# A fused convolution and gated feed-forward kernel: another order of the unit products, another start, and a split last product

## The chip, the cores and the metric

The kernel runs on one core of one Trainium2 chip. The metric is the device time of one execution in microseconds (us), the median of several runs. The core has five engines that work side by side, each with its own in-order queue of instructions: TensorE (PE, matmuls; PEld is its weight load), VectorE (DVE), ScalarE (ACT), GpSimd (POOL) and SyncE (SP, which here issues most DMAs). Matmuls write to PSUM, which has 8 banks of 128 partitions x 512 fp32 numbers.

## The reference

The input x is (8, 4096, 192), fp32. First comes a causal convolution along the sequence with 7 taps, whose weights are a softmax over the taps, one set for each of 8 groups of 24 channels. Then a feed-forward layer follows with a gate between two products:

```python
w = np.exp(w - max); w = w / (sum + 1e-09)
out = np.einsum('hk,bskhg->bshg', w, x_unf)
h = x @ w_in                        # (32768, 192) @ (192, 2048)
g = h * np.clip(h + 3.0, 0.0, 6.0) / 6.0
return g @ w_out                    # (32768, 2048) @ (2048, 192)
```

The weights w_in and w_out arrive as 64-bit numbers and are turned into fp32 on the chip.

## The kernel before, in words

**Blocks.** The 32768 tokens are worked on in 32 blocks of 1024. The 192 channels lie as 64 partitions x 3 "thirds"; partitions 0 to 63 hold the lower 512 tokens of a block, 64 to 127 the upper 512. So a product of the first layer needs 64 rows of TensorE's array, and the lower half (called L, k=0) and the upper half (U, k=1) run side by side on the two halves of its rows (`half_mm`, L303). Such a product is two passes over 512 columns. "OWN" is y, the result of the convolution, in place; "OTHER" is y with the two halves exchanged by DMA (`swap`, L273), so that each half of the rows can also work on the other half's tokens.

**First layer, blocks 1 to 31** (`h_phase`, L404). The layer is done by a scheme of Strassen's kind: seven products P1 to P7 on sums of y (YS1 to YS4, `y_sums`) and of weights (w_in_t), and four plain products K11, K12, K21, K22 for the remaining third. 16 column blocks of w_in make 8 slots, two slots a unit, so 4 units (UNITS), each once for L and once for U. Products of one result add up in one PSUM bank: bank a holds P1, P2, K11; e holds P5; b begins as a copy of P1 and takes P6, P7, P4, K21; f begins as b + p5 and takes P3, K12; d begins as b + p5 and takes K22. A step's name is L or U and an operation: a product; F1, ScalarE's copy of bank a into b (L385), made between P1 and P2 and needed by P6; CE, ScalarE's copy of bank e to SBUF (L388), which gives the bank back; AF and AD, VectorE's sums into f and d (L392); Ra, Rf, Rb, Rd, ScalarE's relu of a result (L317); Ga and so on, VectorE's gate, which writes g and gives the bank back (L321). The string PLAN (L349) is the order in which every unit's steps are issued, and so the order in each engine's queue; a step with ' belongs to the unit before. X (only the first time) is the last store of the block before. Banks are handed out first in, first out (`take`, `give`), so the order of the steps sets which bank a step waits for. After each round GpSimd forms sums of g (`g_sums`).

**Second layer** (`out_strassen`, L586; `out_last`, L546, for the last block). It is of Strassen's kind too: products of 32 output columns each, four side by side on the columns of the array (L427), each over all 128 rows and all 8 slots, two passes each. ScalarE and VectorE (L523, L531) combine the results, VectorE transposes (L537), and SP, at the very end ScalarE too, stores. During this stage VectorE also computes the next block's convolution (L259, L263), and the exchange goes out.

**Block 0** is plain. Its start (from L643) computes the convolution with third 2 on TensorE (diagonal matrices, L661) and thirds 0 and 1 on VectorE in half-width taps, and turns the weights into fp32 unit by unit between: `split` (VectorE, L174 and L178), `clamp` (ScalarE, L186 to L192), `join` (VectorE, L195 and L199, then a GpSimd product, L203). Four pairs of banks are begun early with thirds 0 and 2 (`early`), then third 1. Loop L707 relus and gates; `slots` (L705) says behind which of its 16 steps a weight unit is worked on. Then `out_direct` (L450) does the second layer plainly.

Of the kernel before, what the change touches and what calls it, by code (L numbers as in the profile page):

```python
# [16 lines left out]
def kernel(  # L17
# [316 lines left out]
    def h_out(c, group, bs, between):  # L334
# [14 lines left out]
    PLAN = """  # L349
        LP1 LRd' UP1 LGd' LP4' UP4' URd' LF1 LP5 UGd' UF1 UP5 LP6 UP6 LP2 LCE UCE LRb'  # L350
        UK11 LAF UAF LK11 X URb' UP2 LP7 LGb' UP7 LK12 UP3 UGb' LAD LP3 LRa URa LRf UK12
        UAD UGa LGa LK22 UK22 URf LGf UGf LK21 UK21
    """.split()

# [49 lines left out]
    def h_phase(left):  # L404
        last = None
        for u in range(UNITS + 1):
            now = [Unit(u, k) for k in range(2)] if u < UNITS else None
            for step in PLAN:
                if step == "X":
                    while left:  # L410
                        left.pop(0)()
                    continue
                which = last if step[-1] == "'" else now
                if which:
                    which["LU".index(step[0])].run(step[1:].rstrip("'"))
            if last:
                g_sums(nc.gpsimd, (1, 3), range(2 * u - 2, 2 * u), 2)
            last = now
# [4 lines left out]
    def mm(bank, j, x, w, q, ps_, first, last):  # L423
# [4 lines left out]
                out=bank[j * QS : (j + 1) * QS], lhsT=w_out[:, p, w, cols], rhs=x[:, p],  # L428
# [13 lines left out]
    def store_rows(i, k, q, xt, j, dma=nc.sync):  # L442

        t0 = i * TB + k * N
        dma.dma_start(
            out=out[t0 : t0 + N, q * QS : (q + 1) * QS].rearrange("(t r) d -> r t d", r=QS),
            in_=xt[j * QS : (j + 1) * QS].rearrange("r (t d) -> r t d", d=QS),
        )
# [46 lines left out]
    def product(bank, j, n, q, ks=every):  # L495
        x, w = prod[n]
        return mm(bank, j, S1 if n == 5 else x, w, q, ks, True, True)
# [35 lines left out]
    def store(i, c, k, half_, qs=range(NQ), queues=(nc.sync,)):  # L533
# [3 lines left out]
        nc.vector.transpose(out=xt[r], in_=c[r])  # L537
        for q in qs:
            store_rows(i, k, half_ * NQ + q, xt, q, queues[q % len(queues)])
# [6 lines left out]
    def out_last(i):  # L546
# [32 lines left out]
        b, bank = three(3, 4, 2)  # L579
        add(u2[:], u2[:], bank[m])  # L580
        store(i, u2, 0, 1, queues=both)
        add(u3[rows(2)], u3[rows(2)], bank[rows(NQ)], ALU.subtract)
        store(i, u3, 1, 0, range(2, 3), queues=both[::-1])
        give(b)
# [58 lines left out]
    with tc.manual_schedule():  # L643
# [6 lines left out]

        thirds = [slice(s, s + 1) for s in range(K3)]
        pe_third = K3 - 1
        b = take()
# [5 lines left out]
        for k in range(KC):  # L659
            nc.scalar.mul(diag[:, k], ident[:], c_sb[:, k : k + 1])  # L660
            nc.tensor.matmul(  # L661
                out=psum[:, b], lhsT=diag[:, k], rhs=x_tiles[0][:, pe_third, k : k + N],
                start=(k == 0), stop=(k == KC - 1),
            )
        conv0 = conv_units(0, thirds[:pe_third], 2)
        per = len(conv0) // pe_third
        for k, u in enumerate(conv0):
# [5 lines left out]
            elif k == per:  # L673
                nc.scalar.copy(out=y[:, pe_third], in_=psum[:, b])
                give(b)
                swap(thirds[0])
                swap(thirds[pe_third])
                load(AHEAD)
                split(1)
                clamp(1)  # L680
            elif k == per + 6:
                split(2)
                join(1)
                clamp(2)
            u()
        swap(thirds[1])
        split(3)
        split(4)
        join(2)
        clamp(3)  # L690


        parts = [(c, group) for p in range(0, NP, 2) for group in (OWN, OTHER)
                 for c in (p, p + 1)]
        early = [(c, group, (take(), take())) for c, group in parts[:4]]
        order = (0, pe_third, 1)
        for c in range(2):
            for slot, group, bs in early:
                if slot == c:
                    for s in order[:2]:  # L700
# [90 lines left out]
```

## Time and profile before

| | us |
|---|---|
| median of 9 runs (2425.64 to 2425.79) | 2425.67 |
| the profiled execution | 2425.67 |
| its span (first to last instruction) | 2423.9 |
| VectorE busy | 2088.7 |
| ScalarE busy | 1066.4 |
| GpSimd busy | 671.3 |
| granted TensorE clock, mean | 0.999 |

How to read it: the span is what the profiler saw of the execution; the rest of the time lies around it. In a line of the timeline stand start, length, engine, line of the code, operation, the tile written and the tiles read, their shapes, and, in brackets, how long the engine had been idle before and what released it. The chain of waits goes back from the last instruction, at each step to what released it. A matmul's end is modelled; its start is recorded.

### The profile page before, as it was taken

How to read it: one execution, taken by the hardware profiler on the slowest of the kernel's cores; microseconds unless marked ns; L12 is line 12 of the kernel's file. 1: busy time of each engine (PE TensorE's matmuls, PEld its weight loads, DVE VectorE, ACT ScalarE, POOL GpSimd, SP SyncE). 2: the span in 40 equal slices, each digit the busy share in tenths (PEclk: the TensorE clock that was granted, in tenths of full speed). 3: DMA queues.
4: the chain of work that ended last, by engine and by line, in shares of the span. 5: the costliest groups of instructions: out<-in, count | busy, mean ns of one | idle time of the engine just before them, and what ended most of it. 6: DMA issues, size and time to landing. Idle time of an engine off the chain costs nothing.

```text
span 2423.9 us, 40261 instructions
## 1 busy us (share of the span) xinstructions
PE 2414.0 (100%) x16468; PEld 1042.4 (43%) x16468; DVE 2088.7 (86%) x2534; ACT 1066.4 (44%) x1827; POOL 671.3 (28%) x280
## 2 busy tenths in 40 slices
PE   9999999999999999999999999999999999999998
PEld 4334444444444444443444444444444444344443
DVE  8788888988888888898888898888898888888886
ACT  7234553345443355433454334543345443355433
POOL 2523321233221333122332223322233312333122
PEclk9999999999999999999999999999999999999999
DMA  5111122201122111221112211122201122111210
GB/s 144 40 28 27 27 40 40 40 17 29 35 40 40 21 33 27 40 40 22 32 27 40 40 34 21 25 40 40 40 17 34 30 40 40 21 33 27 40 27 14
DMA packets 227338, 84.67 MB, mean 35 GB/s; under 512 B 205456, under 2 KB 210576, under 8 KB 227152
## 3 DMA queue, kind: packets, MB, share of 16 engines
q1 hardware_dynamic: 225848, 81.56, 17.1%
q8 instruction: 129, 2.11, 0.4%
q14 instruction: 57, 0.47, 0.1%
q10 hardware_dynamic: 1208, 0.27, 0.1%
q0 software_dynamic: 96, 0.26, 0.0%
HBM read 31.72 MB, written 25.17 MB: 23 GB/s over the span
## 4 chain that ended last, share of the span: by engine, by line
PE 99%; DVE 1%; DMA 0%; issue 0%; ACTq 0%; SPq 0%; DVEq 0%
PE psum L311 51%; PE psum L427 48%; DVE y L263 0%; DMA x<-in_x_dram 0%; DMA y<-y 0%; DVE c L531 0%; ACTq L92 0%; DVE scale L174 0%; DVE y L259 0%; DVE sig L199 0%; DVE scale L195 0%; DVE top L178 0%; DVE xt L537 0%; SPq L276 0%; DVEq L259 0%
## 5 line engine op out<-in xcount | busy, mean ns | idle before, releaser
L427 PE MATMUL psum<-g,w_out 128*32 128x512 f32 x9312 | 1163.6, 592 | 0.0
L311 PE MATMUL psum<-y,w_in 64*128 64x512 f32 x3664 | 958.4, 592 | 2.1 <-DVE y L263 1.9
L487 POOL TENSOR_TENSOR s<-g 128x1024 f32<-128x1024 f32 x124 | 293.6, 2368 | 1658.9 <-DVE g L321 1615.3
L317 ACT ACTIVATE r<-psum,half 128x512 f32<-128x512 f32 x1024 | 634.6, 688 | 241.6 <-PE psum L311 238.7
L427 PEld LDWEIGHTS psum<-g,w_out 128*32 128x32 f32 x9312 | 337.4, 110 | 811.7 <-issue 765.1
L321 DVE SCALAR_TENSOR_TENSOR g<-r,psum 128x512 f32<-128x512 f32 x1024 | 643.1, 681 | 4.5 <-ACT r L317 1.1
L427 PE MATMUL psum<-s,w_out 128*32 128x512 f32 x1488 | 638.5, 592 | 0.0
L311 PEld LDWEIGHTS psum<-y,w_in 64*128 64x128 f32 x3664 | 476.9, 187 | 345.1 <-issue 328.1
L311 PE MATMUL psum<-y,w_in_t 64*128 64x512 f32 x1984 | 610.2, 592 | 0.0
L392 DVE TENSOR_TENSOR psum<-psum,p 128x512 f32<-128x512 f32 x496 | 321.5, 694 | 198.6 <-PE psum L311 194.0
L263 DVE SCALAR_TENSOR_TENSOR y<-x,c_sb,y 128x1536 f32<-128x1536 f32 (+1 forms) x210 | 416.7, 1992 | 6.6
L523 ACT COPY c<-psum 32x512 f32<-32x512 f32 x188 | 108.9, 579 | 600.5 <-PE psum L427 543.2
L311 PEld LDWEIGHTS psum<-y,w_in_t 64*128 64x128 f32 x1984 | 280.1, 187 | 209.0 <-issue 142.2
L487 POOL TENSOR_TENSOR g<-g 128x1024 f32<-128x1024 f32 x124 | 336.6, 2714 | 9.7
L531 DVE TENSOR_TENSOR c<-c,psum 32x512 f32<-32x512 f32 (+1 forms) x187 | 128.1, 685 | 95.7 <-ACT c L523 89.8
L427 PEld LDWEIGHTS psum<-s,w_out 128*32 128x32 f32 x1488 | 162.4, 110 | 1.2 <-issue 1.2
L388 ACT COPY p<-psum 128x512 f32<-128x512 f32 x248 | 135.0, 587 | 61.8 <-PE psum L311 61.1
L385 ACT COPY psum<-psum 128x512 f32<-128x512 f32 x248 | 131.4, 571 | 62.3 <-PE psum L311 53.2
L487 DVE TENSOR_TENSOR g<-s,g 128x2048 f32<-128x2048 f32 x62 | 141.2, 2318 | 2.1 <-PE psum L427 2.1
L487 DVE TENSOR_TENSOR g<-g 128x2048 f32<-128x2048 f32 x62 | 139.4, 2289 | 2.3 <-PE psum L427 1.3
L591 ACT COPY c<-psum 96x512 f32<-96x512 f32 x30 | 17.5, 582 | 188.5 <-PE psum L427 188.5
L596 ACT COPY c<-psum 96x512 f32<-96x512 f32 x30 | 17.5, 583 | 169.9 <-PE psum L427 169.9
(46 smaller groups left out, 432.6 us busy)
## 6 DMA issues: line engine op xcount, KB each, us to landing
out_dram<-xt SPq DMA_DIRECT2D x382, 64.0 KB, 2.0
y<-y SPq DMA_DIRECT2D x62, 384.0 KB, 4.9
x<-in_x_dram SPq DMA_DIRECT2D x55, 388.5 KB, 5.8
stage<-in_moe_w_in_dram SPq DMA_DIRECT2D x16, 192.0 KB, 4.4
stage<-in_moe_w_out_dram SPq DMA_DIRECT2D x8, 384.0 KB, 5.4
x<-in_x_dram SPq DMA_DIRECT2D x7, 384.0 KB
y<-y SPq DMA_DIRECT2D x6, 128.0 KB, 2.3
x<-in_x_dram SPq DMA_DIRECT2D x2, 128.0 KB, 4.5
```

The source lines that it names most:

```text
L263: nc.vector.scalar_tensor_tensor(out=to, in0=x[:, part, k + t : k + t + W], scalar=c, in1=to, op0=ALU.mult, op1=ALU.add,)
L311: nc.tensor.matmul(out=psum[:, b], lhsT=w[r], rhs=y[r, third_of_y], start=start, stop=stop, skip_group_check=onto,)
L317: nc.scalar.activation(r6, h, ACT.Relu, bias=half[:], scale=1.0 / 6.0)
L321: nc.vector.scalar_tensor_tensor(out=out, in0=r6, scalar=1.0, in1=h, op0=ALU.min, op1=ALU.mult)
L385: nc.scalar.copy(out=psum[:, bank["b"]], in_=psum[:, bank["a"]])
L388: nc.scalar.copy(out=self.p5[:], in_=psum[:, bank["e"]])
L392: nc.vector.tensor_tensor(out=psum[:, to], in0=psum[:, bank["b"]], in1=self.p5[:], op=ALU.add)
L427: lambda p=p: nc.tensor.matmul(out=bank[j * QS : (j + 1) * QS], lhsT=w_out[:, p, w, cols], rhs=x[:, p], start=(first and p == ps_[0]), sto ...
L487: engine.tensor_tensor(out=o[:, r], in0=a[:, r], in1=b[:, r], op=op)
L523: nc.scalar.copy(out=dst[rows(q)], in_=src[rows(j)])
L531: nc.vector.tensor_tensor(out=out, in0=x, in1=y, op=op)
L591: nc.scalar.copy(out=p1[:], in_=bank[m])
```

## The change

It has three parts. All arithmetic stays.

1. PLAN is replaced by three orders: FIRST for round 0, SECOND for round 1, OTHERS for rounds 2 to 4 (the last round has only the steps with '). A step with + belongs to the unit after: UP5+ and UCE+ in FIRST are the P5 and CE of U of unit 1, and SECOND has no UP5 and UCE. The other steps stand in another order too.
2. The start of block 0: the last two taps of third 1 go to TensorE (bank b1), the first tap to ScalarE, and an add puts them together; third 2 is exchanged before third 0; the first pair of banks is begun before the taps of third 1; some of the split, join and clamp steps move; other `slots`.
3. The last product in `out_last` (P3 with the last third of P4) is done in two halves of 256 tokens, each with its own bank, sums, transposes and stores.

```diff
@@ -346,11 +346,22 @@
-    PLAN = """
-        LP1 LRd' UP1 LGd' LP4' UP4' URd' LF1 LP5 UGd' UF1 UP5 LP6 UP6 LP2 LCE UCE LRb'
-        UK11 LAF UAF LK11 X URb' UP2 LP7 LGb' UP7 LK12 UP3 UGb' LAD LP3 LRa URa LRf UK12
-        UAD UGa LGa LK22 UK22 URf LGf UGf LK21 UK21
+    FIRST = """
+        LP1 UP1 LP5 UP5 LF1 UF1 UP5+ LP6 LCE UCE UP6 LP2 UCE+ UK11 LAF LK11 UAF X UP2 LP7
+        LRa UP7 LK12 URa LAD UP3 LP3 UAD LGa UK12 LK22 LRf UGa UK22 LK21 URf LGf LRd UK21
     """.split()
+    SECOND = """
+        LP1 UGf' URd' LGd' UP1 LP4' LF1 UGd' UP4' LP5 UF1 LP6 UP6 LCE LRb' LP2 UK11 LAF
+        URb' UAF LK11 UP2 LGb' LP7 UP7 URa UGb' LRa UP3 LK12 LAD UAD UK12 LP3 UGa LK22 UK22
+        LRf LGa URf LK21 UK21 LGf LRd
+    """.split()
+    OTHERS = """
+        UP1 UGf' LP1 URd' LGd' LP4' UP4' UGd' LF1 LP5 UP5 UF1 LP6 UP6 LCE UCE LP2 UK11 LAF
+        LRb' UAF LK11 UP2 URb' LGb' LP7 UP7 URa UGb' LRa LK12 UP3 LAD LP3 UAD UK12 UGa LK22
+        UK22 LRf LGa URf LK21 UK21 LGf LRd
+    """.split()
+    PLANS = [FIRST, SECOND] + [OTHERS] * (UNITS - 1)
     class Unit:
@@ -402,30 +413,30 @@
                 give(b)
     def h_phase(left):
-        last = None
-        for u in range(UNITS + 1):
-            now = [Unit(u, k) for k in range(2)] if u < UNITS else None
-            for step in PLAN:
+        work = {(u, k): Unit(u, k) for u in range(UNITS) for k in range(2)}
+        for u, plan in enumerate(PLANS):
+            for step in plan:
                 if step == "X":
                     while left:
                         left.pop(0)()
                     continue
-                which = last if step[-1] == "'" else now
-                if which:
-                    which["LU".index(step[0])].run(step[1:].rstrip("'"))
-            if last:
+                op = step[1:].rstrip("'+")
+                at = u + (step[-1] == "+") - (step[-1] == "'")
+                if at < UNITS:
+                    work[at, "LU".index(step[0])].run(op)
+            if u:
                 g_sums(nc.gpsimd, (1, 3), range(2 * u - 2, 2 * u), 2)
-            last = now
     def dff_half(k):
         return g[:, :, k // G, k % G]
-    def mm(bank, j, x, w, q, ps_, first, last):
+    def mm(bank, j, x, w, q, ps_, first, last, tokens=slice(0, N)):
         cols = slice(q * QS, (q + 1) * QS)
         return [
             lambda p=p: nc.tensor.matmul(
-                out=bank[j * QS : (j + 1) * QS], lhsT=w_out[:, p, w, cols], rhs=x[:, p],
+                out=bank[j * QS : (j + 1) * QS, tokens], lhsT=w_out[:, p, w, cols],
+                rhs=x[:, p, tokens],
                 start=(first and p == ps_[0]), stop=(last and p == ps_[-1]),
                 tile_position=(0, j * QS),
             )
@@ -439,12 +450,12 @@
     every = range(NP)
-    def store_rows(i, k, q, xt, j, dma=nc.sync):
+    def store_rows(i, k, q, xt, j, dma=nc.sync, tokens=slice(0, N)):
         t0 = i * TB + k * N
         dma.dma_start(
-            out=out[t0 : t0 + N, q * QS : (q + 1) * QS].rearrange("(t r) d -> r t d", r=QS),
-            in_=xt[j * QS : (j + 1) * QS].rearrange("r (t d) -> r t d", d=QS),
+            out=out[t0 + tokens.start : t0 + tokens.stop, q * QS : (q + 1) * QS].rearrange("(t r) d -> r t d", r=QS),
+            in_=xt[j * QS : (j + 1) * QS, tokens].rearrange("r (t d) -> r t d", d=QS),
         )
     def out_direct(i, work):
@@ -492,9 +503,9 @@
         5: (None, T1), 6: (S2, T2), 7: (S3, T3),
     }
-    def product(bank, j, n, q, ks=every):
+    def product(bank, j, n, q, ks=every, **tokens):
         x, w = prod[n]
-        return mm(bank, j, S1 if n == 5 else x, w, q, ks, True, True)
+        return mm(bank, j, S1 if n == 5 else x, w, q, ks, True, True, **tokens)
     def four(*parts):
@@ -530,13 +541,13 @@
     def add(out, x, y, op=ALU.add):
         nc.vector.tensor_tensor(out=out, in0=x, in1=y, op=op)
-    def store(i, c, k, half_, qs=range(NQ), queues=(nc.sync,)):
+    def store(i, c, k, half_, qs=range(NQ), queues=(nc.sync,), tokens=slice(0, N)):
         xt = ot.tile([P, N], F32, name="xt")
         r = slice(qs[0] * QS, (qs[-1] + 1) * QS)
-        nc.vector.transpose(out=xt[r], in_=c[r])
+        nc.vector.transpose(out=xt[r, tokens], in_=c[r, tokens])
         for q in qs:
-            store_rows(i, k, half_ * NQ + q, xt, q, queues[q % len(queues)])
+            store_rows(i, k, half_ * NQ + q, xt, q, queues[q % len(queues)], tokens)
     def sums_tiles():
         return (cs.tile([DH, N], F32, name=f"c{k}") for k in range(6))
@@ -576,12 +587,19 @@
         add(u2[:], u2[:], p5[:])
         add(p5[:], u3[:], p5[:])
         store(i, p5, 1, 1)
-        b, bank = three(3, 4, 2)
-        add(u2[:], u2[:], bank[m])
-        store(i, u2, 0, 1, queues=both)
-        add(u3[rows(2)], u3[rows(2)], bank[rows(NQ)], ALU.subtract)
-        store(i, u3, 1, 0, range(2, 3), queues=both[::-1])
-        give(b)
+        for t in range(0, N, N // 2):
+            b = take()
+            bank = psum[:, b]
+            ts = slice(t, t + N // 2)
+            side_by_side(*[
+                product(bank, j, n, q, tokens=ts)
+                for j, (n, q) in enumerate([(3, 0), (3, 1), (3, 2), (4, 2)])
+            ])
+            add(u2[:, ts], u2[:, ts], bank[m, ts])
+            store(i, u2, 0, 1, queues=both, tokens=ts)
+            add(u3[rows(2), ts], u3[rows(2), ts], bank[rows(NQ), ts], ALU.subtract)
+            store(i, u3, 1, 0, range(2, 3), queues=both[::-1], tokens=ts)
+            give(b)
     def out_strassen(i, conv):
         p1, p2, p4, p5, u2, u3 = sums_tiles()
@@ -648,8 +666,18 @@
             out=c_sb[:], in0=e_sb[:], in1=sm[:].to_broadcast([P, KC]), op=ALU.mult
         )
         thirds = [slice(s, s + 1) for s in range(K3)]
         pe_third = K3 - 1
+        pe_taps = KC - 2
+        x0 = x_tiles[0]
+        def pe_tap(b, part, k, first):
+            nc.tensor.matmul(
+                out=psum[:, b], lhsT=diag[:, k], rhs=x0[:, part, k : k + N],
+                start=(k == first), stop=(k == KC - 1),
+            )
         b = take()
         for _ in range(3):
@@ -658,56 +686,66 @@
             )
         for k in range(KC):
             nc.scalar.mul(diag[:, k], ident[:], c_sb[:, k : k + 1])
-            nc.tensor.matmul(
-                out=psum[:, b], lhsT=diag[:, k], rhs=x_tiles[0][:, pe_third, k : k + N],
-                start=(k == 0), stop=(k == KC - 1),
-            )
+            pe_tap(b, pe_third, k, 0)
+        nc.scalar.mul(y[:, 1], x0[:, 1, 0:N], c_sb[:, 0:1])
+        b1 = take()
+        pe_tap(b1, 1, pe_taps, pe_taps)
+        order = (pe_third, 0, 1)
+        parts = [(c, group) for p in range(0, NP, 2) for group in (OWN, OTHER)
+                 for c in (p, p + 1)]
+        early = {}
+        def begin(c, group):
+            early[c, group] = take(), take()
+            for s in order[:2]:
+                h_mm(c, group, early[c, group], s, order)
         conv0 = conv_units(0, thirds[:pe_third], 2)
         per = len(conv0) // pe_third
-        for k, u in enumerate(conv0):
+        for k, u in enumerate(conv0[: per + 2 * pe_taps]):
             if k == 5:
                 split(0)
                 clamp(0)
             elif k == per - 3:
                 join(0, more=False)
-            elif k == per:
+                split(1)
                 nc.scalar.copy(out=y[:, pe_third], in_=psum[:, b])
                 give(b)
-                swap(thirds[0])
                 swap(thirds[pe_third])
-                load(AHEAD)
-                split(1)
                 clamp(1)
-            elif k == per + 6:
+            elif k in (per, per + 1):
+                if k == per:
+                    swap(thirds[0])
+                    load(AHEAD)
+                    begin(0, OWN)
+                    pe_tap(b1, 1, pe_taps + 1, pe_taps)
+                continue
+            elif k == per + 4:
+                join(1)
                 split(2)
-                join(1)
                 clamp(2)
             u()
+        add(y[:, 1], psum[:, b1], y[:, 1])
+        give(b1)
         swap(thirds[1])
+        join(2)
         split(3)
+        clamp(3)
         split(4)
-        join(2)
-        clamp(3)
-        parts = [(c, group) for p in range(0, NP, 2) for group in (OWN, OTHER)
-                 for c in (p, p + 1)]
-        early = [(c, group, (take(), take())) for c, group in parts[:4]]
-        order = (0, pe_third, 1)
-        for c in range(2):
-            for slot, group, bs in early:
-                if slot == c:
-                    for s in order[:2]:
-                        h_mm(c, group, bs, s, order)
-        for c, group, bs in early:
-            h_mm(c, group, bs, order[2], order)
-        slots = [0, 1, 2, 3, 5, 6, 8, 10, 12, 14]
+        for c, group in ((0, OTHER), (1, OWN), (1, OTHER)):
+            begin(c, group)
+        for c, group in parts[: len(early)]:
+            h_mm(c, group, early[c, group], order[2], order)
+        slots = [0, 1, 3, 4, 6, 7, 9, 10, 12, 13]
         n = 3
         for slot, (c, group) in enumerate(parts):
             first = slot < len(early)
             if first:
-                bs = early[slot][2]
+                bs = early[c, group]
             else:
                 bs = take(), take()
                 for s in range(K3):
```

## The prediction, made before the result was known

> **What bounds the kernel now.** I read the page first: TensorE is busy for the whole span, and the chain of waits is TensorE.
>
> ```profile
> PE 2414.0 (100%) x16468; PEld 1042.4 (43%) x16468; DVE 2088.7 (86%) x2534; ACT 1066.4 (44%) x1827; POOL 671.3 (28%) x280
> PE 99%; DVE 1%; DMA 0%; issue 0%; ACTq 0%; SPq 0%; DVEq 0%
> ```
>
> Next the chain in order of time (start, length, what). It splits the span into a start (25.28 us), block 0 (33.57 + 41.34), 31 equal blocks of 38.57 + 36.19, and a tail.
>
> ```profile
> 22.87 2.36 DMA y<-y
> 25.23 0.04 issue
> 25.28 33.57 PE psum L311 x152
> 58.85 41.34 PE psum L427 x384
> ...
> 249.65 38.57 PE psum L311 x175
> 288.22 36.19 PE psum L427 x336
> ...
> 2381.45 36.23 PE psum L427 x336
> 2417.68 0.02 issue
> 2417.70 0.70 DVE c L531
> ```
>
> A busy TensorE is not a full one, so the third view is the timeline of one block's first stage, then of its end.
>
> ```profile
> 250.79 1.06 ACT L385 COPY psum<-psum 128x512 f32<-128x512 f32 x2 [0.50 <-PE psum L311]
> 251.41 0.29 PEld L311 LDWEIGHTS psum<-y,w_in_t 64*128 64x128 f32 x2 [0.68 <-ACT psum L385]
> 251.90 0.18 PEld L311 LDWEIGHTS psum<-y,w_in_t 64*128 64x128 f32 x1 [0.20 <-ACT psum L385]
> ...
> 256.24 0.25 PEld L311 LDWEIGHTS psum<-y,w_in 64*128 64x128 f32 x2 [0.18 <-issue]
> 256.67 0.25 PEld L311 LDWEIGHTS psum<-y,w_in 64*128 64x128 f32 x2 [0.18 <-issue]
> ```
>
> ```profile
> 287.14 1.08 PE L311 MATMUL psum<-y,w_in_t 64*128 64x512 f32 x3
> 288.15 1.06 PE L427 MATMUL psum<-g,w_out 128*32 128x512 f32 x8
> ```
>
> 256.24 to 256.67: one pass takes 0.429 us, in both halves of the rows at once (L, U); a product is two passes, a slot of 0.858. A first stage is 44 products per half, 88 x 0.429 = 37.75 us; the chain has 38.57. The 0.82 over is at the start. L's P6 waits until 251.41 for the first copy of L385, U's P6 until 251.90 for the second. In single starts, U's P6 was due at 251.405: it loses 0.50, and another 0.105, since the two passes behind a stall stand 0.534 apart. L's P6 was due at 251.398: 0.016 + 0.105 = 0.12. The rest is 0.105 at entry and 0.09 at exit. The second fence shows the result: three passes start at 287.14 (L's last), 287.20 and 287.63 (U's last two: 288.22 less 0.59). U ends 0.49 us after L, and L427, which takes all rows, waits for it.
>
> **What the Trainium skill says.** "TensorE: Matmul & The Clock Gate", The mechanism, lets weight loads overtake but calls matmuls strict FIFO. This trace differs: LP1 and UP1 start at 249.58 together, each with its second pass 0.53 later, so a half's pass overtakes the other half's. UP5+ ahead of LP6 needs just this. "SBUF — State Buffer", Who interferes with whom: a VectorE instruction with two SBUF inputs and a GpSimd one exclude each other. The trace agrees: a tap of 0.48 us took 1.22 when GpSimd multiplied at 12.42 and at 18.46. The first page's What's actually happening says that an idle TensorE gets half the clock; here 14.4 to 19.0 us ran at 0.63. "VectorE: DVE Perf Modes", The TRN2 errata, prices an fp32 tensor_tensor at (N+151)/0.96 ns; N=512 gives 691 and the trace has 684.
>
> **The order of the units (31 blocks).** Nothing is added: UP5 of unit 1 moves into unit 0, its copy UCE with it; no DMA moves, and the X store stays behind both AFs on VectorE. The new order of U is P1, P5, P5+, P6. By the trace's starts P5+ runs at 251.405 and P6 at 252.263. The copy UF1 ends at 251.85, so U no longer waits: 0.603 gone. Next late is L: its 0.12 stays, since P1, P5, P6 and LF1 stand as before. L already ended 0.49 before U, so L427 starts 0.49 earlier. The seventh bank that UP5+ takes was freed in the last stage; the bank that VectorE frees last is only the eighth. U then runs one product ahead: FIRST has 10 products in L and 11 in U, SECOND 11 and 10, OTHERS 11 each, and the last round adds P4' to both: 44 each, so both halves stay filled.
>
> Laid on the slots with the trace's durations, the tight places are these. In SECOND U has P1, P4', P6: P1's end comes 1.018 after its start (0.429 + 0.589), the copy starts 0.09 later, takes 0.572, and the load follows 0.05 later: 1.73 against two slots, 1.716. So U pays 0.015 + 0.105 = 0.12 there, which is free: L is 0.12 behind. In OTHERS UF1 writes the bank that UGd' frees; I get 0.05 to 0.17 us of margin for UP6, and as much for UP7 and UK22 behind AF and AD. Bounds for the block: at best the 0.603 whole, at worst more is lost in units 1 to 3 than gained (rival 3). I take 0.49: 31 x 0.49 = 15.2 us.
>
> **The start.** Before, the path is third 1: taps on VectorE until 22.30, exchange landed at 25.23, TensorE at 25.28. VectorE loses 6 of its 14 half taps (0.396 apart: 2.4 us) and gains one add (0.68). Tap 0 goes to ScalarE, where it waits for x, landed at 9.38: about 0.67 us by L317's 0.688, so clamp(0) ends near 11.9, not 10.65, and GpSimd's first product starts near 12.6, not 12.42. split(1), 0.54, now lies before third 0's last taps, and these wait for GpSimd: third 0 is ready near 14.83 instead of 14.26. From there: two taps 15.5, join(1) 0.94, split(2) 0.54, six taps 2.4 and GpSimd's exclusion 0.6, the add: 20.8. The exchange takes 2.9 as before: 23.75. TensorE's queue: third 2 in OWN at 13.8, third 0 at 14.9, the tap to 16.65, third 2 in OTHER (exchanged from 13.1, landed near 16.0) to 17.5, third 0 in OTHER from 17.75 to 18.7. Then 12 passes and 4 more (1, OTHER and thirds 1) at 0.429 after join(1), hence (0, OTHER)'s third 1 at about 23.85: 1.43 earlier, without the 0.105 of restart. SP issues the exchange of third 2 before third 0 and load(4) behind both; unit 4's words land near 20 and are split after 22. Before, 76 passes took 33.57 us where 32.6 would do; three stalls of that were banks waiting for gates (at 32.7, 35.1, 38.0). The new slots spread the ten splits and joins; by 2.68 us of VectorE for a slot with a unit, 1.20 without, I get TensorE's end of this stage 1.75 earlier. Its cover is the clock: at 0.63, as before, TensorE would be late and the start gains nothing. Its idle time before 14.4 shrinks from 1.9 us to about 0.8, since a tap of third 1 runs in it, so I take full clock and 1.6; bounds 0 and 2.3. The last w_out unit was ready at 67.2; TensorE needs it 12.0 into L427's stage, near 69.1.
>
> **The tail.**
>
> ```profile
> 2416.23 0.71 DVE L537 STREAM_TRANSPOSE xt<-c 96x512 f32<-96x512 f32 x1
> 2417.70 0.68 DVE L531 TENSOR_TENSOR c<-c,psum 96x512 f32<-96x512 f32 x1 [0.77 <-PE psum L427]
> 2418.42 0.71 DVE L537 STREAM_TRANSPOSE xt<-c 96x512 f32<-96x512 f32 x1
> 2419.16 0.69 DVE L531 TENSOR_TENSOR c<-c,psum 32x512 f32<-32x512 f32 x1
> 2419.89 0.70 DVE L537 STREAM_TRANSPOSE xt<-c 32x512 f32<-32x512 f32 x1
> ```
>
> VectorE is full until 2416.94 and idles 0.77; so halves that TensorE ends early can't start early. Four instructions become eight. By the skill's price less the 7 ns it is over, an add of 256 takes 0.417, a transpose 0.44 (0.707 less the same 0.267), each 0.033 apart: 8 make 3.69, end 2420.63 against 2420.59. The last stores are half as large: 0.1 gained. Passes of 256 columns occur nowhere; 0.215 by width, 0.429 at worst. VectorE needs the second half at 2418.8, TensorE ended at 2417.6: 1.2 of cover, so the worst costs 6.9 - 1.2 = 5.7 us, the best nothing.
>
> **Sum.** 15.2 + 1.6 + 0.1 = 16.9. The profiled execution took 2425.67 us (span 2423.9 and 1.8 around it), which is the median too: 2408.8.
>
> **Rivals.** (1) TensorE keeps its queue in order, and LP6 starts only behind both passes of UP5+: L loses 0.429 more, 0.06 per block remains: 31 x 0.06 + 1.7 = 3.6, so 2422.1. For it: the page; against it: the starts above. (2) A part of the wait moves to UP6, UP7 or UK22 of units 1 to 3, small as the margins are: two restarts of 0.105 and some waiting beyond the free 0.12, about 0.2 a block: 2415.0. For it: margins of 0.05; against it: in the kernel before, loads released 0.25 us and less ahead of their slot (after AF, AD) cost nothing. (3) Slower: UK22, URd, UGd', UF1, UP6 is a chain through one bank and returns in each unit, so U's lateness doesn't relax it. Late by e, it costs e + 0.105 in three units, less 0.12; from e = 0.10 it eats the 0.49. At 0.2 it is 0.80, so 31 x 0.31 - 1.7 = 7.9 slower: 2433.6. For it: VectorE is busy nearly 5 of 5 us at 263 and 273; against it: its idle 2 us beside those.
>
> **Numbers.** Forecast 0.72, rival 1 0.06, rival 2 0.17, rival 3 0.05. The range takes the forecast with its bounds (2406.8, with a full gain at the start and 0.53 a block, to 2412) and most of rival 2: 2406.8 to 2417. A measurement tells 0.2%, 4.85 us, from no change: forecast and rival 2 are faster, 0.88, with some of the rest of rival 2 near the edge; rival 1 same, 0.07; slower 0.05.
>
> **What would show it.** Right: the chain's first stages at 38.08 instead of 38.57, no load released by L385 later than L's, L and U ending within 0.15 us; the first long stage near 23.9, L427's first near 57.1; eight VectorE instructions after 2416.94's counterpart. Wrong: a stall on VectorE's gates or L392 once per unit; LP6 on top of UP5+'s second pass; a clock below 1 from 15 to 19 us.

## The result and the profile after

The changed kernel takes 2410.37 us (median of 9 runs, 2410.28 to 2411.16), against 2425.71 (median of 29 runs beside them): the ratio is 0.9937, with a 95% interval of 0.9929 to 0.9945. That is 15.3 us less; the forecast was 16.9 less. The profiled execution took 2409.94 us, its span is 2408.2.

The page of the changed kernel: busy time and share of each engine, then the shares in the chain of waits.

```profile
PE 2400.3 (100%) x16536; PEld 1023.2 (42%) x16536; DVE 2089.4 (87%) x2533; ACT 1078.4 (45%) x1828; POOL 672.6 (28%) x280
PE 99%; DVE 0%; DMA 0%; SPq 0%; ACT 0%; issue 0%; DVEq 0%; ACTq 0%
```

TensorE still sets the time; what shrank is time inside it that its busy share hides. The chain in order of time (start, length, what) shows where. L427 of before is L437 here, L385 is L396, L392 is L403, L531 is L542 and L537 is L548.

```profile
17.35 40.81 PE psum L311 x184
58.16 41.34 PE psum L437 x384
99.50 38.10 PE psum L311 x175
173.78 38.43 PE psum L311 x174
248.40 38.08 PE psum L311 x174
286.47 36.19 PE psum L437 x336
...
1733.69 38.28 PE psum L311 x175
```

A first stage takes 38.08 instead of 38.57. Two of the 31 take longer (38.43 and 38.28); which ones do is not the same in every profile. The second stages are unchanged at 36.19. Taken from single starts on TensorE, the spans differ as follows:

| piece | before | after | gained |
|---|---|---|---|
| start of the span to L437's first matmul in block 0 | 58.78 | 58.09 | 0.69 |
| 31 first stages (28 of them 38.571 and 38.077) | | | 14.66 |
| L437's first in the last block to the end | 42.52 | 42.15 | 0.37 |
| sum (2423.9 - 2408.2) | | | 15.7 |

The timeline of the changed kernel at the start of the block that begins at 248.40:

```profile
249.53 1.06 ACT L396 COPY psum<-psum 128x512 f32<-128x512 f32 x2 [0.49 <-PE psum L311]
250.15 0.29 PEld L311 LDWEIGHTS psum<-y,w_in_t 64*128 64x128 f32 x3 [0.24 <-ACT psum L396]
250.64 0.18 PEld L311 LDWEIGHTS psum<-y,w_in_t 64*128 64x128 f32 x1 [0.20 <-ACT psum L396]
251.12 1.05 PEld L311 LDWEIGHTS psum<-y,w_in 64*128 64x128 f32 x5
```

Before, the second load released by the copies came 0.50 us behind its due time and U stood still. Here it comes at 250.64 while U is still busy with P5+, and the P6 that needs it starts on time, at 251.01. And at the end of the stage:

```profile
285.45 1.02 PE L311 MATMUL psum<-y,w_in_t 64*128 64x512 f32 x4
286.40 1.06 PE L437 MATMUL psum<-g,w_out 128*32 128x512 f32 x8
```

Four last passes stand together, their single starts at 285.449, 285.456, 285.878 and 285.885: L and U end 0.007 us apart, where U had been 0.49 behind.

### The profile page after: what moved, and what is told of

Read it like the earlier page. It is cut to its first block, busy times and chain, and to the rows that moved or that the text cites. A ratio compares the mean times of both kernels' runs of the same rounds, so it can differ in the third digit from the quotient of the medians.

```text
span 2408.2 us, 40221 instructions
## 1 busy us (share of the span) xinstructions
PE 2400.3 (100%) x16536; PEld 1023.2 (42%) x16536; DVE 2089.4 (87%) x2533; ACT 1078.4 (45%) x1828; POOL 672.6 (28%) x280
## 4 chain that ended last, share of the span: by engine, by line
PE 99%; DVE 0%; DMA 0%; SPq 0%; ACT 0%; issue 0%; DVEq 0%; ACTq 0%
PE psum L311 51%; PE psum L437 48%; DVE c L542 0%; DMA x<-in_x_dram 0%; DMA out_dram<-xt 0%; DVE xt L548 0%; SPq L103 0%; SPq L137 0%; DVE top L178 0%; PE psum L676 0%; DVE y L263 0%; SPq L92 0%; ACT y L690 0%; ACT scale L189 0%; ACT c L534 0%
## 5 line engine op out<-in xcount | busy, mean ns | idle before, releaser
L437 PE MATMUL psum<-g,w_out 128*32 128x512 f32 (+1 forms) x9376 | 1163.7, 589 | 0.0
L311 PE MATMUL psum<-y,w_in 64*128 64x512 f32 x3664 | 884.7, 591 | 0.5 <-DVE y L263 0.3
L317 ACT ACTIVATE r<-psum,half 128x512 f32<-128x512 f32 x1024 | 642.1, 689 | 241.0 <-PE psum L311 233.9
L437 PEld LDWEIGHTS psum<-g,w_out 128*32 128x32 f32 x9376 | 339.5, 110 | 810.0 <-issue 765.6
L437 PE MATMUL psum<-s,w_out 128*32 128x512 f32 x1488 | 638.5, 592 | 0.0
L311 PEld LDWEIGHTS psum<-y,w_in 64*128 64x128 f32 x3664 | 440.2, 187 | 366.0 <-issue 290.6
L311 PE MATMUL psum<-y,w_in_t 64*128 64x512 f32 x1984 | 524.8, 592 | 0.0
L403 DVE TENSOR_TENSOR psum<-psum,p 128x512 f32<-128x512 f32 x496 | 324.6, 694 | 195.7 <-PE psum L311 186.8
L311 PEld LDWEIGHTS psum<-y,w_in_t 64*128 64x128 f32 x1984 | 248.9, 186 | 192.9 <-issue 123.4
L542 DVE TENSOR_TENSOR c<-c,psum 32x512 f32<-32x512 f32 (+2 forms) x189 | 128.4, 679 | 81.2 <-ACT c L534 76.0
L396 ACT COPY psum<-psum 128x512 f32<-128x512 f32 x248 | 138.8, 571 | 71.9 <-PE psum L311 57.1
L437 PEld LDWEIGHTS psum<-s,w_out 128*32 128x32 f32 x1488 | 162.4, 110 | 1.2 <-issue 1.2
```

What stands on the lines that cost most here:

```text
L311: nc.tensor.matmul(out=psum[:, b], lhsT=w[r], rhs=y[r, third_of_y], start=start, stop=stop, skip_group_check=onto,)
L317: nc.scalar.activation(r6, h, ACT.Relu, bias=half[:], scale=1.0 / 6.0)
L396: nc.scalar.copy(out=psum[:, bank["b"]], in_=psum[:, bank["a"]])
L403: nc.vector.tensor_tensor(out=psum[:, to], in0=psum[:, bank["b"]], in1=self.p5[:], op=ALU.add)
L437: lambda p=p: nc.tensor.matmul(out=bank[j * QS : (j + 1) * QS, tokens], lhsT=w_out[:, p, w, cols], rhs=x[:, p, tokens], start=(first and p ...
L542: nc.vector.tensor_tensor(out=out, in0=x, in1=y, op=op)
```

## The experiments

### The parts one at a time

**e1** has part 1 alone: the three orders, FIRST to OTHERS, in the kernel before.

```diff
+    PLANS = [FIRST, SECOND] + [OTHERS] * (UNITS - 1)
...
+                at = u + (step[-1] == "+") - (step[-1] == "'")
```

> The kernel before with part 1 alone: the three orders FIRST, SECOND and OTHERS with UP5 of unit 1 in unit 0; start and tail as before. Theory (the time came from U's wait for the second copy at the head of each of 31 blocks): the traces show the stage from first L311 to first L427 at 38.57 us before and 38.08 after in nearly all blocks, so 31 x 0.49 less the two or three blocks with another stall, 14.7 us: 2411.0 us, from 2410.4 to 2411.7. Rival (the start and the tail carry several us of it, and the blocks less): above 2413 us.

Measured: 2410.87 us (2410.84 to 2410.93), ratio 0.9939 (0.9925 to 0.9952). First stages 38.08, block 0 and the tail as before (58.79 and 42.52). So 14.8 of the 15.3 us come from the orders.

**e2** has part 2 alone, the new start.

```diff
+        nc.scalar.mul(y[:, 1], x0[:, 1, 0:N], c_sb[:, 0:1])
+        b1 = take()
+        pe_tap(b1, 1, pe_taps, pe_taps)
...
-        slots = [0, 1, 2, 3, 5, 6, 8, 10, 12, 14]
+        slots = [0, 1, 3, 4, 6, 7, 9, 10, 12, 13]
```

> The kernel before with part 2 alone: the new start of block 0 and the new slots. Theory from the two traces: the first L427 comes 0.69 us earlier (58.09 instead of 58.78) and nothing else moves: 2425.0 us, from 2424.7 to 2425.4. Rival (the start is worth the 1.6 us of the prediction and part of it is given back in block 1): first L427 still at 58.1 but the time at or above 2425.6; or the start alone gives 1.6: 2424.1 us.

Measured: 2425.67 us, median of 13 runs (2425.20 to 2425.74), ratio 0.9999 (0.9991 to 1.0008). In the profiled execution (2425.28 us) L427's first comes at 58.07, 0.70 earlier than before, but ten of the thirteen times lie above 2425.5 and three below 2425.3. The usual execution gains next to nothing. This is where the forecast lost most.

**e3** has part 3 alone, the split last product.

```diff
-        b, bank = three(3, 4, 2)
...
+        for t in range(0, N, N // 2):
```

> The kernel before with part 3 alone: the last product in two halves of 256 tokens. Theory from the two traces: the end lies 42.18 us behind the last block's first L427 instead of 42.5, since the smaller last stores land sooner, though the last transpose waits 0.45 us for a store: 2425.4 us, from 2425.2 to 2425.6. Rival (256-column passes cost more than half of 512-column ones, and the tail loses): 2425.8 us or more.

Measured: 2425.34 us (13 runs, 2425.30 to 2425.51), 0.37 less than before; the tail is 42.16 against 42.52. The three parts by themselves give 14.8 + 0.0 + 0.4 = 15.2 of the 15.3, so they do not help or hurt each other by anything that matters.

### The move without the search, and the search without the move

**e4** keeps the order of before and only moves UP5 and UCE of unit 1 into round 0.

```diff
-        LP1 LRd' UP1 LGd' LP4' UP4' URd' LF1 LP5 UGd' UF1 UP5 LP6 UP6 LP2 LCE UCE LRb'
+        LP1 UP1 LF1 LP5 UF1 UP5 UP5+ LP6 UP6 LP2 LCE UCE UCE+
...
+        LP1 LRd' UP1 LGd' LP4' UP4' URd' LF1 LP5 UGd' UF1 LP6 UP6 LP2 LCE LRb'
```

> The kernel before with UP5 and UCE of unit 1 moved into unit 0 (UP5+ behind UP5, UCE+ behind UCE) and every other step of the old order left where it was. Theory (the moved product is what closes the gap, and the new search only keeps the later units free of waits): most of the gain is there, 0.3 to 0.49 us a block, 2410.5 to 2416 us, with what is missing shown as loads that wait on VectorE or ScalarE in units 1 to 3. Rival (with U one product ahead, the old order holds U's or L's queue up in every unit, and the new order is what makes the move pay): less than 0.15 us a block, above 2421 us.

**e5** is the opposite: the new orders, with UP5 and UCE back in unit 1.

```diff
-        LP1 UP1 LP5 UP5 LF1 UF1 UP5+ LP6 LCE UCE UP6 LP2 UCE+ UK11 LAF LK11 UAF X UP2 LP7
+        LP1 UP1 LP5 UP5 LF1 UF1 LP6 LCE UCE UP6 LP2 UK11 LAF LK11 UAF X UP2 LP7
...
-        LP1 UGf' URd' LGd' UP1 LP4' LF1 UGd' UP4' LP5 UF1 LP6 UP6 LCE LRb' LP2 UK11 LAF
+        LP1 UGf' URd' LGd' UP1 LP4' LF1 UGd' UP4' LP5 UP5 UF1 LP6 UP6 LCE UCE LRb' LP2 UK11 LAF
```

> The kernel before with the three new orders, but P5 and CE of U of unit 1 back in unit 1 (no UP5+ and UCE+), start and tail as before. Theory (the moved product alone fills the first gap; the search only spares waits that U's lead brings): U waits for its second copy again, L427 starts 38.5 us after the first L311, 2425 to 2426.5 us. Rival (the new order of the steps is itself worth the 0.19 us a block by which the move in the old order, 38.27, falls short of 38.08): 38.38 a block, 2419.8 us or less.

e4 takes 2416.78 us (2416.70 to 2416.87), ratio 0.9963 (0.9951 to 0.9976); e5 2425.64 (2425.61 to 2425.76), ratio 1.0 (0.9992 to 1.0008). Their chains in order of time, e4 first:

```profile
249.10 38.27 PE psum L311 x176
```

```profile
249.73 38.56 PE psum L311 x175
```

The search alone brings 0.01 us a block, the move alone 0.30, both together 0.49. In e4 the single starts show where the other 0.19 is. U no longer waits at 251.4, but at 269.08 a pass stands 0.08 late and the next one 0.104 more (0.533 instead of 0.429 behind it). Its load at 269.08 starts 0.05 us behind the end of VectorE's gate at 269.03. By that distance, the one that a load keeps from its releaser elsewhere, it had waited for the gate. That is a wait of the second rival's kind: at this gate no pass stands late in the kernel before, where U is behind anyway, and here it costs 0.08 + 0.10 a block. In e1 this stall is absent, and in e5 U's wait behind the second copy is back (0.917 between two starts of U at 251.98, in the kernel before 0.928).

### What the new start gives

These versions are all the changed kernel with one edit, e12 apart.

**e8** takes the slots of before.

```diff
-        slots = [0, 1, 3, 4, 6, 7, 9, 10, 12, 13]
+        slots = [0, 1, 2, 3, 5, 6, 8, 10, 12, 14]
```

> The changed kernel with the old list of slots in block 0. Theory (the earlier exchange of third 1 brings nothing by itself, since VectorE's first gate starts at 25.00 us instead of 25.07; the even slots bring the 0.69 us of the profile): the first L427 is back at 58.6 to 58.8 us. Rival (the earlier TensorE start brings it, whatever the slots): the first L427 stays within 0.2 us of 58.09.

**e9** lets the first two relus go ahead of clamp(3) in ScalarE's queue.

```diff
         split(3)
-        clamp(3)
         split(4)
...
-            h_out(c, group, bs, (lambda: None) if first else between)
+            h_out(c, group, bs, (lambda: clamp(3) if slot == 0 else None) if first else between)
```

> The changed kernel with ScalarE's clamp of weight unit 3 moved behind the first two relus of block 0. Theory (in the changed kernel the first relu waits until 24.28 us behind that clamp though its bank is full at about 21.9, and gates, join(3) and GpSimd's unit 3, which TensorE waits for until 28.90, all follow from it): the first gate at about 24.2 instead of 25.00, no load released by GpSimd or by a gate between 28 and 33 us, first L427 at 57.3 to 57.6 instead of 58.09, and the time down by 0.5 to 0.7 us beside the changed kernel. Rival (TensorE is bound by the exchange of third 1 alone): first L427 within 0.15 us of 58.09.

**e10** spreads the slots: from step 1 on no two weight units are in neighbouring steps until the last three.

```diff
-        slots = [0, 1, 3, 4, 6, 7, 9, 10, 12, 13]
+        slots = [0, 1, 3, 5, 7, 9, 11, 13, 14, 15]
```

> The changed kernel with slots = [0, 1, 3, 5, 7, 9, 11, 13, 14, 15]: the same ten weight units, but fewer of them ahead of step 11, and no two joins next to each other. Theory (ScalarE bounds block 0's first stage: two relus of 0.57 and three clamps of 0.63 to 0.65 make 3.05 us for a step with a unit against TensorE's 2.57; and a GpSimd product that gets in between two adjacent joins costs 0.5 us in most executions): no gate stall after 34 us, first L427 at 57.2 to 57.7 us instead of 58.57 in the usual execution and 58.09 in the profiled one, 2409.2 to 2409.7 us beside 2410.37. Rival (VectorE's gates or the exchange bound it): first L427 at 58.0 or later, 2410.1 us or more. Rival (the weights of the second layer come late): L427's first stage longer than 41.34 us.

**e12** is the kernel before with the slots of e10 and nothing else.

> The kernel before with slots = [0, 1, 3, 5, 7, 9, 11, 13, 14, 15] alone. Theory (ScalarE is the bound of this stage already before, so the slots help without the new start): TensorE starts the stage at 25.28 as before and needs 32.8 us: first L427 at 58.0 to 58.3 instead of 58.78, 2425.0 to 2425.3 us. Rival (the slots only help behind the earlier exchange): 2425.6 us or more.

Measured, with the first relu on ScalarE (L317) and the first matmul of the second layer (L427 or L437) in block 0:

| version | median us | first relu | second layer starts | between |
|---|---|---|---|---|
| before | 2425.71 | 24.363 | 58.778 | 34.42 |
| after | 2410.37 | 24.284 | 58.091 | 33.81 |
| e8, old slots | 2410.72 (2410.25 to 2410.92) | 24.161 | 58.643 | 34.48 |
| e6, below | 2410.14 (2410.05 to 2410.32) | 24.280 | 58.566 | 34.29 |
| e9, relus first | 2411.46 (2411.40 to 2411.56) | 23.523 | 59.608 | 36.09 |
| e10, wide slots | 2410.22 (2410.08 to 2410.34) | 24.297 | 58.114 | 33.82 |
| e12, before with wide slots | 2425.00 (2424.92 to 2425.22) | 24.318 | 58.110 | 33.79 |

With the old slots (e8) the stretch is as long as before, though the rest of the new start is there; with the new ones it is 33.8 in one profile and 34.3 in another of the same start, of which more below. The medians need care here: part of a time lies outside the span, and in e8 that part was 1.8 us in two executions and 2.4 to 2.6 in three. By their spans (2408.3 to 2408.5) e8's executions are no longer than those of the changed kernel (2408.5 to 2408.7, the profiled one 2408.2). So a gain from the new slots shows in the profile of the changed kernel, but not in its usual execution.

The forecast let TensorE's earlier start carry through to the end of the stage. That start came as planned: third 1's exchange lands at 24.24 instead of 25.23. But e12 keeps the old start, and its chain shows TensorE waiting for that exchange:

```profile
22.83 2.33 DMA y<-y
25.16 0.04 issue
25.20 32.98 PE psum L311 x152
58.18 1.83 PE psum L427 x13
```

Though TensorE begins this stage 0.9 us later than in e10, the second layer begins at the same 58.11: with these slots the new start brings nothing there. TensorE's weight loads in e10 show where it loses its lead:

```profile
28.91 0.72 PEld L311 LDWEIGHTS psum<-y,w_in 64*128 64x128 f32 x5 [0.39 <-POOL w_in L203]
...
31.57 0.29 PEld L311 LDWEIGHTS psum<-y,w_in 64*128 64x128 f32 x2 [0.30 <-DVE g L321]
32.17 24.76 PEld L311 LDWEIGHTS psum<-y,w_in 64*128 64x128 f32 x117 [0.30 <-DVE g L321]
```

It waits for weight unit 3 and for the gates of the third step, and from 32.17 on it loads for 24.76 us without such a wait. In e12, where TensorE comes later, the load behind the second of these gates starts at 32.17 as well. In single starts, the last held-up pass stands at 32.70 in both, and from there it is 25.41 us to the second layer in both, in e11 and in the profile of the changed kernel. A TensorE that comes earlier only waits longer at this place. The gates in turn follow ScalarE: in e10 the first gates of the first three steps start at 25.01, 27.92 and 30.83, each 0.03 us behind the end of their relu. ScalarE's busy time in block 0's first stage before, in a window (length, busy time and instructions, granted clock, DMA share, GB/s):

```profile
25.30:58.80 33.50, 32.86 (x59) 1.00 0.51 141
```

Of 33.50 us, 32.86 are busy: in this one stage, an engine that is busy 44% of the span is full. In the changed kernel it is 32.16 of 32.80. The share alone does not show what the gates wait for, since VectorE, which makes them, is nearly as busy (32.38 and 32.05 in the same windows); that they start right behind their relus does, for the first three steps. What ScalarE does there, in its timeline of before:

```profile
22.60 0.61 ACT L186 ACTIVATE sig<-scale,bias_e 128x384 f32<-128x384 uint32 x1 [3.54 <-DVE scale L174]
23.25 0.62 ACT L189 ACTIVATE scale<-sig,bias_e 128x384 uint32<-128x384 f32 x1
23.90 0.56 ACT L192 ACTIVATE sig<-stage 128x384 f32<-128x384 uint32 x1
24.36 1.25 ACT L317 ACTIVATE r<-psum,half 128x512 f32<-128x512 f32 x2
...
27.26 1.24 ACT L317 ACTIVATE r<-psum,half 128x512 f32<-128x512 f32 x2
```

and after:

```profile
22.53 0.61 ACT L186 ACTIVATE sig<-scale,bias_e 128x384 f32<-128x384 uint32 x1 [3.51 <-DVE scale L174]
23.18 0.62 ACT L189 ACTIVATE scale<-sig,bias_e 128x384 uint32<-128x384 f32 x1
23.83 0.56 ACT L192 ACTIVATE sig<-stage 128x384 f32<-128x384 uint32 x1
24.28 1.26 ACT L317 ACTIVATE r<-psum,half 128x512 f32<-128x512 f32 x2
...
27.20 1.25 ACT L317 ACTIVATE r<-psum,half 128x512 f32<-128x512 f32 x2
```

A step of loop L707 with a weight unit is two relus (0.57 from start to start) and the three instructions of a clamp (0.65, 0.64 and 0.47): 2.9 us from 24.36 to 27.26. The releaser of the first line is VectorE's split(3), and the first relus queue behind clamp(3). VectorE is through with third 1 a full us earlier (its add ends at 21.29; the last tap of before at 22.30), but join(2), 0.94 us, now stands ahead of split(3), which thus starts at 22.14 instead of 22.22. So the first relu moves by 0.08 us and not by 0.99.

e9 shows that the first relu alone isn't it either, against its expectation: at 23.52 it is 0.76 earlier, but clamp(3) and the next clamp then stand together behind it, the second pair of relus comes at 28.24 instead of 27.20, and the gates behind these end at 29.64 and 30.23, where TensorE's loads wait until 29.75 and 30.29. The median is 1.1 us above the changed kernel's. Relus and clamps share one full engine: the gates wait for the first, the weights for the second. e10 had been expected to gain more than it did (57.2 to 57.7 for the second layer), because ScalarE was taken for the bound of the whole stage; with these slots TensorE is, past the third step.

### Why one execution of the new start differs from another

**e6** gives the output tile seven buffers instead of four, which concerns the tail (below); its start is that of the changed kernel.

```diff
-        ot = ctx.enter_context(tc.tile_pool(name="ot", bufs=4))
+        ot = ctx.enter_context(tc.tile_pool(name="ot", bufs=7))
```

> The changed kernel with 7 buffers instead of 4 for xt, the tile that the stores read. Theory (the last transpose of the changed kernel waits 0.45 us because its xt is one that a store has not finished reading): that wait is gone and the end comes 0.4 us sooner, 2409.9 to 2410.1 us beside 2410.37. Rival (the last landing, not the transpose, sets the end, or the wait is one of the order of stores and not of the buffer): 2410.3 us or more.

Measured: 2410.14 us (2410.05 to 2410.32). But in its profile the second layer starts at 58.566, in that of the changed kernel at 58.091, with the same instructions in the same order up to there. The two part at 35 us, in two neighbouring steps with a join each (slots 3 and 4). VectorE's timeline in e6, then in the changed kernel:

```profile
34.69 0.56 DVE L195 SCALAR_TENSOR_TENSOR scale<-stage,scale 128x384 uint32<-128x384 uint32 x1
35.16 1.36 DVE L199 SCALAR_TENSOR_TENSOR sig<-top,sig 128x384 f32<-128x384 uint32 x1
36.45 1.27 DVE L321 SCALAR_TENSOR_TENSOR g<-r,psum 128x512 f32<-128x512 f32 x2
```

```profile
34.68 0.57 DVE L195 SCALAR_TENSOR_TENSOR scale<-stage,scale 128x384 uint32<-128x384 uint32 x1
35.15 0.57 DVE L199 SCALAR_TENSOR_TENSOR sig<-top,sig 128x384 f32<-128x384 uint32 x1
35.62 1.30 DVE L321 SCALAR_TENSOR_TENSOR g<-r,psum 128x512 f32<-128x512 f32 x2
```

GpSimd's product of the join before starts at 34.86 in both. In e6 L199 is held up (1.36 instead of 0.57 us), and the gates behind come 0.83 later; in the changed kernel's profile L199 is not, and GpSimd's product takes 1.73 us instead of 1.25. "SBUF — State Buffer", Who interferes with whom, of the Trainium skill says that the two exclude each other and that issue order decides who blocks; the trace agrees in that one of the two is longer each time, and here the same start falls on either side. The late gates reach TensorE as a late load in e6:

```profile
36.56 0.19 PEld L311 LDWEIGHTS psum<-y,w_in 64*128 64x128 f32 x1 [0.24 <-issue]
37.24 0.29 PEld L311 LDWEIGHTS psum<-y,w_in 64*128 64x128 f32 x2 [0.49 <-issue]
37.77 0.72 PEld L311 LDWEIGHTS psum<-y,w_in 64*128 64x128 f32 x5 [0.24 <-DVE g L321]
```

where the changed kernel loads from 35.52 to 38.71 without a gap. The difference at the end of the stage, 58.566 - 58.091 = 0.48 us, fits the medians: the changed kernel's is 0.43 above its profiled execution. So the 0.69 of the table above is the better course of the start, and the usual one should gain about 58.78 - 58.57 = 0.2; e2's median shows 0.04 of it, and where the rest went is open. That one and the same program takes both courses is read from its times, since only one execution of a version has a trace: e2's thirteen times fall into the two groups given above, and the changed kernel's profiled 2409.94 stands apart from its other nine.

With e10's slots no two joins are neighbours there; its five times lie within 0.26 us, and it was at 58.11 in its profile.

### A version that is faster than both

**e11** adds to e10 the seven buffers of e6, and moves ScalarE's tap of third 1, which waits for x until 9.44 us, behind clamp(0).

```diff
-        nc.scalar.mul(y[:, 1], x0[:, 1, 0:N], c_sb[:, 0:1])
...
             if k == 5:
                 split(0)
                 clamp(0)
+                nc.scalar.mul(y[:, 1], x0[:, 1, 0:N], c_sb[:, 0:1])
```

> The changed kernel with these slots, 7 buffers for xt and the tap that ScalarE computes behind the clamp of unit 0 instead of ahead of it. Theory: the slots as above, 0.25 us at the end from the buffers, and 0.1 to 0.4 us because unit 0 and third 0 are no longer held up by ScalarE's wait for x until 9.44 us: 2408.7 to 2409.4 us. Rival (the tap's place is indifferent, the exchange of third 1 hangs on VectorE's count): the difference to the run with the slots alone is the 0.25 us of the buffers.

**e13** is e11 with the weight units on even steps.

```diff
-        slots = [0, 1, 3, 5, 7, 9, 11, 13, 14, 15]
+        slots = [0, 2, 4, 6, 8, 10, 12, 13, 14, 15]
```

> The run with slots, buffers and the later tap again, with slots = [0, 2, 4, 6, 8, 10, 12, 13, 14, 15], so that the first two steps of block 0 are not both followed by a unit. Theory (ScalarE's chain of relu, relu, clamp from the first relu on, 2.91 us a step with a unit, sets when the gates of step 2 free the banks of TensorE's step 6): the relus of step 2 start near 28.0 instead of 29.74 us, TensorE's wait at 31.7 us is gone, the one for unit 3 at 28.4 stays, and the first L427 comes at 56.9 to 57.3 us instead of 57.73: 2408.2 to 2408.7 us beside 2409.05. Rival (the bound is TensorE's own start, by exchange and bank): first L427 within 0.15 us of 57.73.

e11 takes 2409.05 us (2408.81 to 2410.14), ratio to before 0.9932 (0.9918 to 0.9946); e13 2408.84 (2408.75 to 2409.56), ratio 0.9931 (0.9917 to 0.9944). In e11 the first relu comes at 23.94 instead of 24.30, and the second layer at 57.73 instead of 58.11: what ScalarE gains at its front arrives whole at the end. (The exchange lands 0.34 earlier as well, but e12 shows that it is not what counts.) In e13 the stretch between is 33.50 (23.951 to 57.446), 0.3 less than in e11. One wait of TensorE's loads remains early in the stage, here in e13's timeline:

```profile
27.98 0.19 PEld L311 LDWEIGHTS psum<-y,w_in 64*128 64x128 f32 x1 [0.24 <-issue]
28.57 0.72 PEld L311 LDWEIGHTS psum<-y,w_in 64*128 64x128 f32 x5 [0.41 <-POOL w_in L203]
```

It waits for weight unit 3, which is through GpSimd only then. e13 is 1.5 us under the changed kernel, and no time of the one reaches those of the other; against e11 its 0.2 us is less than the spread of their times, and by their spans (2407.0 to 2407.1 in both) the two do not differ. e13's second layer had been expected at 57.3 or earlier. Splitting unit 3 ahead of join(2) was not tried.

## Why the prediction was right, and where it was wrong

**The orders** (15.2 predicted, 14.8 by e1, 14.66 between the traces): right in mechanism and size. U's 0.603 is gone, L's refill of 0.105 stays, and a stage is 38.077 where 38.08 was expected. The missing 0.5 us has two causes. The first stage of block 1 had been only 38.52 before, so it gained 0.42; and the two stages of 38.43 and 38.28 gave back 0.35 and 0.21. The free 0.12 that U has against L is used: in unit 1 two of U's starts stand 0.495 and 0.46 apart instead of 0.429. The loads before them wait for UF1 and for UAF, which are just in time, as the working of SECOND had it for the first and the margin behind AF for the second.

**Rival 1** (TensorE in order, 2422.1) fell: L's P6 and U's P5+ start 0.002 us apart in the block at 248.40 of the changed kernel, and their passes alternate from there, though UP5+ stands first in the program: one half's passes do not wait for the other half's. **Rival 2** did not come true in this order, but e4 shows it real in another, at 0.19 a block and for a gate. **Rival 3**, the chain through one bank that is late in every unit, does not show in any first stage.

**The start** (1.6 predicted; 0.69 in the profiled execution, 0.04 by e2's median, about 0.2 by the course seen in e6): this term was mis-sized, and it is nearly the whole error. The step that failed is the price of the 16 steps of block 0, "by 2.68 us of VectorE for a slot with a unit, 1.20 without". ScalarE was not priced, though each such step costs it 2.9 us, and the first relu, from which its first steps follow one another, moved by only 0.08. The Trainium skill has the price: "ScalarE: Activation LUTs", What ACT_TABLE_LOAD costs, gives 280 ns and 0.833 ns an element for an activation with a bias operand, so 600 ns for 384, where the trace has 0.61, and 707 for 512, where it has 0.69. Added up for a step with the trace's own durations, that is more than VectorE's 2.68: an estimate of 0.61 + 0.62 + 0.56 + 2 x 0.69 = 3.2 us before overlap. The events that lead to the exchange came out close: the add ended at 21.29 (20.8 predicted, though the terms given for it add up to 20.7), the exchange landed at 24.24 (23.75). About 0.3 of this 0.5 was there by third 0 already, ready at 15.11 and not 14.83, since VectorE's L178 took 1.16 us beside GpSimd's product instead of 0.35: the prediction let only instructions with two SBUF inputs be held up. The clock was right. The same window in the trace before, then after (length; busy time and instructions of PE, PEld, DVE, ACT, POOL; clock):

```profile
14.40:19.00 4.60, 4.59 (x14) 1.72 (x16) 4.60 (x14) 3.51 (x6) 0.54 (x1) 0.63 0.67 160
```

```profile
14.40:19.00 4.60, 4.33 (x18) 1.48 (x16) 4.60 (x11) 2.40 (x5) 1.32 (x1) 1.00 0.76 187
```

The full clock was there, and was worth as little as the rest of TensorE's gain.

**The tail** (0.1 predicted, 0.37 between the traces and by e3). VectorE's last eight instructions in the changed kernel's timeline, of which the last four:

```profile
2403.46 0.42 DVE L542 TENSOR_TENSOR c<-c,psum 96x256 f32<-96x256 f32 x1
2403.91 0.44 DVE L548 STREAM_TRANSPOSE xt<-c 96x256 f32<-96x256 f32 x1
2404.38 0.42 DVE L542 TENSOR_TENSOR c<-c,psum 32x256 f32<-32x256 f32 x1
2405.26 0.43 DVE L548 STREAM_TRANSPOSE xt<-c 32x256 f32<-32x256 f32 x1 [0.45 <-DMA out_dram<-xt]
```

Durations are as worked out (0.417 and 0.44), and a pass of 256 columns takes 0.216 us. Two terms were missed, of opposite sign. The last transpose waits 0.45 for a buffer that a store still reads; with seven buffers (e6) the wait is gone and the tail is 41.95 instead of 42.15, half of the 0.4 that was expected. And the end of the span is 2.5 us behind the last transpose, where it was 3.3 (2.7 in e6, where that transpose does not wait): behind stores of half the size the end comes 0.6 to 0.8 sooner, not 0.1.

In all: 16.9 = 15.2 + 1.6 + 0.1 became 15.3 = 14.8 + 0.0 + 0.4 by the parts' own medians, 0.1 of it unassigned. The time lies in the range.

## What to carry to other kernels

Price every engine in the stage that you change, not the one that you watch: an engine that is at 44% over the span can be full in one stage, and then an earlier transfer or a faster clock elsewhere can bring nothing. A full engine need not be the bound, though: follow the loads that wait to what released them. Moving independent work into a gap removes the gap only if the gates behind it are also in time; lay the whole order on the slots again, for the next late release costs its lateness plus a refill. When a profiled execution and the median differ by more than the spread of the times, look for two instructions that exclude each other and start within a few hundred nanoseconds, here 0.3 us; but compare the spans first, for part of a time lies outside the span.

## What the runs showed of the hardware

- The same start can take two courses in block 0, 0.48 us apart, by which of VectorE and GpSimd is held up (L199 at 35.15: 0.57 us in the changed kernel's profile, 1.36 in e6's).
- Now and then a stage is 0.2 to 0.35 us longer: none to two of the 31 in each profile, in different blocks. In e2 the copy L385 at 1521.27 started about 0.28 us behind its place in other blocks, with nothing in the trace to hold it. The cause stays open.
- A pass that a wait has held up costs up to another 0.105 us: the next pass of its half starts 0.534 behind it instead of 0.429 (the changed kernel at 250.15, e4 at 269.08); where the load was just in time, it was 0.495 and 0.46.
- One half's passes do not wait for the other half's that stand before them in the program (LP6 and UP5+, 0.002 us apart).
